# Kernel rows and their gradients by pairs of channels in a fused S4 convolution and gated FFN, forward and backward

## The chip, the core and the metric

The kernel runs on one core of one Trainium2 chip, as one program. The core has five engines, each with its own instruction queue: TensorE (PE, with its weight loads shown as PEld), VectorE (DVE), ScalarE (ACT), GpSimd (POOL) and SyncE (SP, which here only issues DMAs). The metric is the device time of one execution in microseconds; several executions are timed and the median is given. One further execution is recorded by the hardware profiler, and all rows of profiles and traces below come from that one.

## The reference

Inputs are a sequence `u` of 2048 tokens by 512 channels, the parameters of an S4 layer (`A`, `B`, `C` as real and imaginary parts, 512 channels by 128 states, `log_dt` and `Dskip` by channel), two FFN weights (512 x 1792 and 1792 x 512) and a gradient of the output. The outputs are the forward result and eleven gradients. Cut to what matters:

```python
xn = layernorm(u)
dt = exp(log_dt)[:, None];  dB = dt * (B_re + 1j*B_im)
P  = exp((dt * (A_re + 1j*A_im))[:, :, None] * arange(L))      # channel, state, time
K  = einsum("dn,dnl,dn->dl", C, P, dB).real                    # the kernel row of each channel
s  = irfft(rfft(xn padded) * rfft(K padded))[:L] + xn * Dskip  # a causal convolution
g  = silu(silu(xn @ w1) @ w2)
out = u + s * g
# and the gradients of out by u, A_re, A_im, B_re, B_im, C_re, C_im, log_dt, Dskip, w1, w2
```

For the change two parts matter: the kernel rows `K`, and on the way back the gradients by `A`, `B`, `C` and `dt` that come from the gradient of `K`.

## The kernel before, in words

All large products are bf16 with f32 sums in PSUM, a block of 128 partitions at a time. The convolution is done by DFTs on TensorE (a step of 128-point products at line 405, transposes at 415, a second step at line 425, and the way back at 440 and 453), the FFN by plain products (751, 768; backward 1149, 1169, 1202, 1231).

**Kernel rows.** The power of a state at time `e + 8 j` is the product of two, one of 32 powers `8 j` (tile `Y`) and one of 21 exponents `e` (tile `E`, `NE = 21`); times in between take the row of a neighbour when `KE` is filled. With the states on the partitions, the sum over states is then a matmul of `Y` (weights) by `E` times the coefficients (tile `W`). Channels are taken by four: the weights hold `(j, a)`, 32 x 4 = 128 columns, where `a` is the channel within the four, and the moving side holds `(e, a)`, 21 x 4 = 84 columns. Only the quarter in which both `a` agree is wanted. There are four terms (real and imaginary, two exponent halves), so `gen_kernel_rows` issues 16 products for every four fours of channels into one PSUM tile `ps_k` (128 x 336), and copies that to `Xr`. It does this for 4 blocks of 128 channels, 2 halves, 2 groups of 8 fours, 2 parts of a group: 512 products and 32 copies. Then `group` picks the wanted quarter: products with 0/1 matrices `SEL[kind, a]`, one for each `a`, summed over `a` into `ps_e`, which also moves rows between the 128 partitions where an exponent wraps. The rows are copied to `KE` and by DMA to the layout of the DFT (`Kb`).

**Their gradients.** `gen_ssm_fold` reads the gradient of the rows (four DMAs a block, one for each `a`), folds it with 0/1 matrices `FO` (line 953) and copies it with the last dimension repeated four times to `Gf`. `gen_ssm_v` multiplies `Gf` by a mask `MK` that leaves for each partition `(j, a)` the columns of its own `a` (`Gb`, 128 x 2688 elements), and multiplies the transposed powers `YT` by it: per four channels and per real or imaginary part one product of 168 columns into `ps_v` (line 998), four products into one PSUM tile of two banks, which is then copied to `Vb` (256 products, 64 copies). `gen_ssm_products` multiplies by `E` (`Tp`, line 1013), `gen_ssm_sums` adds over the exponents with an identity matrix (1031 to 1035), `gen_ssm_grads` turns the sums into the gradients.

**Order.** Every part is a Python generator that issues a few instructions and yields. Each has a letter, and a string `PLAN` of seven stages says which generator goes on next, so it sets the order of the instructions in every engine's queue: stage 1 set-up (begins at 0 us), stage 2 kernel rows `R`, powers `P` and `Q`, forward convolution `X` and `C`, FFN forward `F` (about 60 to 212 us), stages 3 and 4 the convolution backward and the FFN backward, stages 5 and 6 the gradients of the rows (`N`, `Y`, `V`, `T`, `S`, `Z`) beside the weight gradients (`t`, `w`, `v`), stage 7 the layer norm backward. `WAYS` says for each copy out of PSUM of a letter whether ACT (`A`) or DVE (`D`) does it (`k.ev`, lines 112 and 113). `SLOTS` says which buffer a tile takes. Products of a stage use PSUM pools `pf` (3 buffers), `pc` (2) and `pt` (1); `ps_k`, `ps_e` and `psS` share the one of `pt`, `ps_v` uses `pc`.

One form in this kernel already uses less than the full width of TensorE: the second DFT step (line 425) has weights of 64 columns and writes its results to partitions 0 to 63 and 64 to 127 in turn.

Of the kernel before, what the change touches and what calls it, by code (L numbers as in the profile page):

```python
# [18 lines left out]
P = 128  # L19
# [8 lines left out]
222127p33355553317511p333366565577077700071076676JJ17677p77747767676677F7FF777F6777477677FF77F77FFp77FF67766F667FF6F6FF8  # L28
4466666644468886685JJ8888/QFFFFFFJJXXXXFFFFXXPPFFXFXPXFPP9PFFFFFXXFFFXXPQFFQJXXQQQQQQXQJFPXPXQPQRXFFPPRRXRXXPFFFXRFRFRXR
PRQQQPQFFQQQQRFFXXQFQQRRRRPPXXFFFFFFFRRJRXFXRRRPPRUXXRRPXXXRRQRQQFQQFXXXRRRXRRQRRPRQQQQJFFQXXPPRFFFFFFPRRPPFFFCCCCCFXCFR  # L30
RRRCFFCFFFFFRFRCCQQQQQQFRRCRRCCQQQFFFQCCCCPFFFRRCCCCRRFQRCFXXXRRXPCCCRPCCQFCXPXFFQCRURFFXFRQQQCCXRCFQFFFCCQPQQFFFFCRRCQF
XFXPPRRXRRFXXXJXQRRXFRRCCXXPRRPPJJPRCRCXRPFQRCCCQXXPCJCCQFFFQQFFFRFCCPPFFCCQFRQFFQQXFQCXQFFCFFFRRRCFFCCRRCJCCRRCCCRCRCPC
RCRXXFFQRCRXXXQQCRCXRCCXCXRQQRRRRXRQRXQQXQQFXRXPFXXXFFFCJCPFRFPPCCCCFFRRPPFXRQRRRFFFXUFQQQFFXCCFCCFQFCRRCUCQCCCFRQQRCCQR
QFCQFCCRRCCRRRRRCCRCCRRCRCCCCRRFFFFCRCCCCCRRRCRRCCRC/FCCCCFFCCCCCFGGFGGCCCCCGGGGGGFGFGCCCCGGGGGFFCFFFFFCFCCFFGWGGCCCCHHF
FGGGCCCCCFGCCFFCCCCCWCCCCHWGGWWWCCCHHHHHWWCWWWCCWCCWDMWWWDGDDWWDWWDDDWLWWWWDWDDDLCLLLMMMMDDDWWDD/dDDaDaddDDdDsAAAEADDDDD
BAaBAAaABBDEaAAsADDDAsABBBAABBBoooAoAAABBBsAAAEDBBADBlDBDAlAlBBBBBxBDABBBBOAooAxxDDoBDBABoAAOBBEBOBOOOOOlldlxaBxxBooBBBo
sxOooBBBBDDDDxoxoxBdDaxBBDBAABBBdBBBDDAAaBBBBOBBBBBBAABBsAAAOADDDEDAAADBAADOOoBsOdOBABOBAoAoAAABBBDoxAOAOODBABosBBABDxDB
BAoOBDDDDAADDAAODxDDooodDAOOOdoBBaOBBOBoBBoOOdodDDxDEDxxBxaBBBsAAAOOaAABBABABBDBDAABDBDBoBoBBxxDOOExDDDsxAABBxBABBaBABBs
AAABBABBEOOOxOxBAABBBABBABAxBBBxxaaaBBBBBAsBBBBBBBBBBBBAAAxxBBBAAABBBBBAAAABBBABdBd/xxdAdNssxxsYaAsAAAAYYNAAAAAAAxxNNAAA
AAAAAAYAAAAAANNxVVVVAAxVVVVVVAATTVVxxVVxVVYxVVTYYxxxxNNNTTTTNSVVVVVVVYxSx/VTTSTSVTTVVVVVhhVVVSSVVVVVVVTTTYYttTtSthVTTNTT  # L40
# [31 lines left out]
d=DDADAAAA;  # L72
B=AADAADAAAAAADAAAAAAAAAAAAAAAAAADDADAAADAAAAAAAAAAAAAADDA;
x=ADADAAADDADADDAA;
V=ADDADDADADDADADAAAAAAADDAAAAADAAADAAAAAAAAAAADAAAAAAAAAAAAAAADAA;
w=DADDDDAAAAAAAA;
v=DADADDDAADDAAAAAAAAADAAADAAA"""

# [1366 lines left out]
```

## Time and profile before

| | us |
|---|---|
| median of 3 runs | 607.65 |
| lowest, highest | 607.44, 610.42 |
| the profiled execution | 606.76 |
| its span, first to last instruction | 605.0 |
| PE busy in it | 560.1 |
| DVE busy | 533.0 |
| ACT busy | 443.2 |
| POOL busy | 77.5 |

The mean TensorE clock granted in the span is 0.989 of full speed. A row of a group gives line, engine, operation, the tiles written and read, the shapes and the count, then busy time and the mean of one in ns, then the engine's idle time just ahead of them with what ended it. A row in order of time gives start and length in us of a series of equal instructions. Lengths of matmuls overlap, so their cost in a series is read from start to start. A row of a stretch gives its bounds, its length, and busy time with counts for PE, PEld, DVE, ACT and POOL, then clock, DMA share and GB/s.

### The profile page before, as it was taken

What the parts mean: (1) busy time and instruction counts of PE and PEld (TensorE: products, weight loads), DVE (VectorE), ACT (ScalarE), POOL (GpSimd) and SP (SyncE); (2) the same over time, 40 slices, a digit from 0 to 9 for tenths busy, and PEclk for the clock granted to TensorE, in tenths of its full rate; (3) what the DMA queues carried; (4) which work ended last, traced back from release to release, by engine and by line L of the source; (5) the groups of instructions that cost most, each with busy time, mean ns of one, the idle gap of its engine ahead of it and who ended that gap; (6) DMA issues with size and microseconds to landing.
All of it is one profiled execution on the core that took longest, in us unless ns stands there. A gap on an engine that the chain in (4) does not pass through costs nothing. (4 is left out here: it accounts for less than half of the span.)

```text
span 605.0 us, 14383 instructions
## 1 busy us (share of the span) xinstructions
PE 560.1 (93%) x5861; PEld 425.3 (70%) x5884; DVE 533.0 (88%) x906; ACT 443.2 (73%) x552; POOL 77.5 (13%) x171
## 2 busy tenths in 40 slices
PE   1597989999999989999999999999799999999995
PEld 1354758677777686786787767775787888795864
DVE  8989999999999889999998799568759889978894
ACT  7989989999998669998787864641575456434661
POOL 6211001010101120000000100000000202123121
PEclk9988999999999999999999999999999999999998
DMA  9896678676658598959877798797999999999993
GB/s 267 260 306 203 254 245 287 225 249 236 248 160 331 216 297 322 330 126 294 276 232 250 233 296 253 210 230 181 242 202 207 232 252 150 246 207 270 309 242 132
DMA packets 156066, 146.83 MB, mean 243 GB/s; under 512 B 79520, under 2 KB 133024, under 8 KB 152416
## 3 DMA queue, kind: packets, MB, share of 16 engines
q1 hardware_dynamic: 146688, 123.10, 72.1%
q0 software_dynamic: 6768, 19.93, 9.2%
q10 hardware_dynamic: 2544, 2.88, 1.5%
q8 instruction: 46, 0.75, 0.5%
q14 instruction: 20, 0.16, 0.1%
HBM read 63.44 MB, written 62.00 MB: 207 GB/s over the span
## 5 line engine op out<-in xcount | busy, mean ns | idle before, releaser
L112 ACT CAST dA<-ps_s 128x1024 bf16<-128x1024 f32 x86 | 86.3, 1037 | 7.6 <-PE ps_s L425 4.0
L751 PE MATMUL ps_h<-XT,W 128*128 128x256 bf16 x448 | 57.4, 279 | 6.2 <-ACT hT L112 4.6
L112 ACT CAST Vb<-ps_v 128x672 bf16<-128x672 f32 x49 | 34.1, 723 | 37.3 <-PE ps_v L998 32.7
L1149 PE MATMUL ps_da<-doT,W 128*128 128x256 bf16 x448 | 55.2, 273 | 1.2 <-ACT pd_s L112 1.1
L1013 DVE TENSOR_TENSOR Tp<-Vb,Eb 128x1344 bf16<-128x1344 bf16 x64 | 51.0, 850 | 5.9 <-ACT Vb L112 5.9
L768 PE MATMUL ps_o<-W,aT 128*128 128x512 bf16 x214 | 52.7, 399 | 1.1 <-issue 0.9
L112 ACT CAST dB<-ps_i 128x1024 bf16<-128x1024 f32 x41 | 41.1, 1031 | 16.4 <-PE ps_i L440 15.6
L751 PEld LDWEIGHTS <-W 128*128 128x128 bf16 x448 | 43.6, 100 | 12.9 <-issue 7.3
L1231 PE MATMUL ps_w<-dh_tok,xn 128*128 128x256 bf16 x448 | 51.8, 273 | 0.1
L1169 PE MATMUL ps_dx<-W,dhT 128*128 128x512 bf16 x224 | 50.8, 379 | 0.0
L1202 PE MATMUL ps_w<-YD,a_tok 128*128 128x512 bf16 x214 | 49.8, 379 | 0.5
L440 PE MATMUL ps_i<-I,sp_in 128*128 128x256 bf16 x384 | 47.3, 273 | 1.7 <-ACT dB L112 1.7
L1149 PEld LDWEIGHTS <-W 128*128 128x128 bf16 x448 | 42.8, 98 | 8.0 <-issue 2.8
L1231 PEld LDWEIGHTS <-xn 128*128 128x128 bf16 x448 | 43.2, 98 | 5.9 <-issue 0.5
L1152 DVE TENSOR_TENSOR dhT<-ps_da,dhT 128x512 bf16<-128x512 f32 x56 | 37.2, 684 | 10.3 <-PE ps_da L1149 7.3
L440 PEld LDWEIGHTS <-sp_in 128*128 128x128 bf16 x384 | 37.0, 98 | 8.9 <-DVE dB L113 1.9
L768 PEld LDWEIGHTS <-aT 128*128 128x128 bf16 x224 | 22.0, 102 | 29.3 <-issue 7.9
L1169 PEld LDWEIGHTS <-dhT 128*128 128x128 bf16 x224 | 21.3, 98 | 24.2 <-issue 1.2
L1202 PEld LDWEIGHTS <-a_tok 128*128 128x128 bf16 x224 | 21.5, 98 | 23.2
L466 DVE TENSOR_TENSOR cm<-sp_in,dA 128x2048 bf16<-128x2048 bf16 x24 | 29.3, 1219 | 4.9 <-DMA sp_in<-KXd 3.3
L425 PE MATMUL ps_s<-dB,F 128*64 128x512 bf16 x192 | 28.2, 388 | 3.8 <-ACT dB L112 2.1
L571 ACT ACTIVATE sn<-V 128x2048 bf16<-128x2048 int16 (+1 forms) x16 | 30.5, 1905 | 1.1 <-DVE V L567 1.1
(241 smaller groups left out, 1254.2 us busy)
## 6 DMA issues: line engine op xcount, KB each, us to landing
Yd<-YD SPq DMA_DIRECT2D x8, 1024.0 KB, 4.9
sp_in<-Ud SPq DMA_DIRECT2D x8, 1024.0 KB, 7.3
h_in<-Hd SPq DMA_DIRECT2D x14, 512.0 KB, 5.1
Ed<-E SPq DMA_DIRECT2D x8, 672.0 KB, 3.9
Eb<-Ed SPq DMA_DIRECT2D x8, 672.0 KB, 5.4
Hd<-hT POOLq DMA_DIRECT2D x8, 512.0 KB, 6.1
Ud<-dA SPq DMA_DIRECT2D x4, 1024.0 KB, 5.2
KXd<-dA SPq DMA_DIRECT2D x4, 1024.0 KB, 4.3
```

The lines of the kernel that those rows point to most:

```text
L112: return self.nc.scalar.copy(out=out, in_=in_)
L440: nc.tensor.matmul(out=ps[:, g], lhsT=Y[:, c, g0 + g, :], rhs=k.I2[:, c].rearrange("p c m -> p (c m)"), start=(c == 0), stop=(c == 1))
L466: TT(out=t2[:], in0=b[:, :, gs], in1=a[:, 1:2, gs].to_broadcast([P, 2, n, P]), op=ALU.mult)
L571: nc.scalar.activation(out=sn[:, 0:n], in_=low, func=ACT.Sin, scale=-2 * PI_LO / 2.0 ** PB)
L751: nc.tensor.matmul(out=ps[:, j], lhsT=k.W1[:, dk, ft * P:ft * P + P], rhs=XTv[:, :, dk, :], start=(dk == 0), stop=(dk == DK - 1))
L768: nc.tensor.matmul(out=ps[:], lhsT=aT[:, ft, t * P:t * P + P], rhs=k.W2[:, ft, :], start=(ft == 0), stop=(ft == FT - 1))
L1013: k.nc.vector.tensor_tensor(out=Tp[:, c, :, r ^ c].rearrange("p e (q w) a -> p q w e a", w=2), in0=Vb[:, :, c].rearrange("p q w (e a) -> p ...
L1149: nc.tensor.matmul(out=ps[:, j], lhsT=k.W2[:, ft, dk * P:dk * P + P], rhs=dTv[:, :, dk, :], start=(dk == 0), stop=(dk == DK - 1))
L1152: nc.vector.tensor_tensor(out=dh[:, i0:i0 + 2, :], in0=ps[:], in1=dh[:, i0:i0 + 2, :], op=ALU.mult)
L1169: nc.tensor.matmul(out=ps[:], lhsT=dhs[ft // 8][:, ft % 8, t * P:t * P + P], rhs=k.W1[:, :, ft * P:ft * P + P], start=(ft == 0), stop=(ft ...
L1202: nc.tensor.matmul(out=ps[:], lhsT=at[:, t, :], rhs=k.do[:, t, :], start=(t == 0), stop=(t == k.T - 1))
L1231: nc.tensor.matmul(out=ps[:], lhsT=k.xn[:, t, dk * P:dk * P + P], rhs=dh[:, t].rearrange("p j n -> p (j n)"), start=(t == 0), stop=(t == k ...
```

## The change

Channels are taken by two instead of four, in both directions.

In `gen_kernel_rows` the weights are now `(j, a)` with two values of `a`, 64 columns, and the moving side `(e, a)` has 42. Each old product becomes two, one for each pair `z` of the four channels, and these write to partitions 0 to 63 and 64 to 127 of the same PSUM tile. `ps_k` holds eight fours instead of four (128 x 336 again), so there are 1024 products and 16 copies. Half of the result is wanted instead of a quarter, so `SEL` has two matrices for each kind, and `group` issues half as many products. Since the partitions now hold `(z, j, a)`, the 0/1 matrices are built from a permuted identity `pairs`.

In the gradients the last dimension of `Gf`, `MK` and `Gb` is two, so `Gb` has 1344 elements instead of 2688. Each product of line 998 becomes two, one for each half `z` of the partitions (64 rows of the weights and of the moving side each, 84 columns), written to the two banks of `ps_v`. The copy to `Vb` has as many elements as before, with `z` reordered. `Vb`, `Tp`, `E` and `Y` have the same sizes with rows of two instead of four in the last dimension. The gradient of the rows is read by the same four DMAs to other partitions.

`PLAN`, `SLOTS` and `WAYS` are all new: the order of the whole program differs. Stage 2 has 611 letters instead of 626, stage 3 159 for 163, stage 4 467 for 466, stage 5 117 for 109, stage 6 397 for 405.

```diff
-R=AAAAAAADAADDADAAAAAAAAAAAAAAAADDDDDDDDAADAADAAAAADDAAAAADAAAAAADAAAAAAADAAAADDA;
+R=AAADAADDAADAAAAAAAAAAADDAADDDDADAAAAAAAADDDDAADAAAAAAAAAAADAADA;
...
-V=ADDADDADADDADADAAAAAAADDAAAAADAAADAAAAAAAAAAADAAAAAAAAAAAAAAAADAA;
+V=AADADAADADDADADAAADDADADAAADDDDDAADDAAAAAAADADAAAAAAAAAAAAAADDAA;
...
-F=AADAAAAAAAAADAAADAAAAAAAAAAADDAAAAAAADADAAAADAAADAAAAAAAADDAADADDDDDDDAA;
+F=AADAAAAAAAADDAAAAAAAAAAAAAAAAAAAAAAAADADAAAADAAADAAAAAAADDAAAAADDADDDDAA;
...
-    k.SEL = k.p1.tile([P, 4, 4, 128], BF16, name="SEL")
+    k.SEL = k.p1.tile([P, 4, 2, 128], BF16, name="SEL")
...
+    G.memset(w.pairs[:], 0.0)
+    G.affine_select(out=w.pairs[:], in_=w.pairs[:], compare_op=ALU.not_equal, fill=1.0,
+                    base=0, pattern=[[2, 32], [64, 2], [1, 2]], channel_multiplier=-1)
...
-            W = tbl.tile([P, 4, 8, NE, 4], BF16, name="W", tag="W", bufs=2)
+            W = tbl.tile([P, 4, 16, NE, 2], BF16, name="W", tag="W", bufs=2)
...
-            for u in range(2):
-                ps = k.pt.tile([P, 4, 84], F32, name="ps_k", tag="pt")
-                for q in range(4):
-                    for m in range(4):
-                        nc.tensor.matmul(out=ps[:, q], lhsT=Y[:, m % 2, q0 + 4 * u + q].rearrange("p j a -> p (j a)"),
-                                         rhs=W[:, m, 4 * u + q].rearrange("p e a -> p (e a)"), start=(m == 0), stop=(m == 3))
-                yield
-                qq = 16 * h + q0 + 4 * u
-                k.ev(Xr[:, :, :, qq:qq + 4], ps[:].rearrange("p q (e a) -> p a e q", a=4))
-                yield
+            ps = k.pt.tile([P, 8, NE * 2], F32, name="ps_k", tag="pt")
+            for q in range(8):
+                for m in range(4):
+                    for z in range(2):
+                        nc.tensor.matmul(out=ps[64 * z:64 * z + 64, q], lhsT=Y[:, m % 2, 2 * (q0 + q) + z].rearrange("p j a -> p (j a)"),
+                                         rhs=W[:, m, 2 * q + z].rearrange("p e a -> p (e a)"), start=(m == 0), stop=(m == 3))
+                if q % 4 == 3:
+                    yield
+            qq = 16 * h + q0
+            k.ev(Xr[:, :, :, qq:qq + 8], ps[:].rearrange("p q (e a) -> p a e q", a=2))
+            yield
...
-        n = len(terms) * 4
+        n = len(terms) * 2
...
-            for a in range(4):
+            for a in range(2):
                 nc.tensor.matmul(out=o, lhsT=k.SEL[:, kind, a], rhs=Xr[:, a, e0:e1, :], start=(i == 0), stop=(i == n - 1))
...
-    Gf = sb.tile([P, 32, NE, 4], BF16, name="Gf", tag="Gf", bufs=2)
+    Gf = sb.tile([P, 32, NE, 2], BF16, name="Gf", tag="Gf", bufs=2)
...
-            Gb = sb.tile([P, 16, 2, NE * 4], BF16, name="Gb", tag="Gb", bufs=2)
+            Gb = sb.tile([P, 16, 2, NE * 2], BF16, name="Gb", tag="Gb", bufs=2)
...
-                    nc.tensor.matmul(out=ps[:, u, 168 * c:168 * c + 168], lhsT=YT[:, c, q + u, :],
-                                     rhs=Gb[:, q0 + q + u].rearrange("p w x -> p (w x)"), start=True, stop=True)
-            yield
-            k.ev(Vb[:, q:q + 2].rearrange("p q c w x -> p q (c w x)"), ps[:, :, 0:336])
+                    for z in range(2):
+                        zs, x0 = slice(64 * z, 64 * z + 64), 168 * u + 84 * c
+                        nc.tensor.matmul(out=ps[:, z, x0:x0 + 84], lhsT=YT[zs, c, q + u, :],
+                                         rhs=Gb[zs, q0 + q + u].rearrange("p w x -> p (w x)"), start=True, stop=True)
+            yield
+            k.ev(Vb[:, 2 * q:2 * q + 4].rearrange("p (u z) c w x -> p z u (c w x)", z=2),
+                 ps[:, :, 0:336].rearrange("p z (u x) -> p z u x", u=2))
...
-        Tp = sb.tile([P, 2, NE, 2, 16, 4], BF16, name="Tp", tag="Tp", bufs=2)
+        Tp = sb.tile([P, 2, NE, 2, 32, 2], BF16, name="Tp", tag="Tp", bufs=2)
```

## The prediction

> **What bounds the kernel now.** I read the page first (busy shares, the span in slices), then busy time by stretch, then the groups and the order in time of the tiles that the change touches, then the waits. The page's shares:
>
> ```profile
> PE 560.1 (93%) x5861; PEld 425.3 (70%) x5884; DVE 533.0 (88%) x906; ACT 443.2 (73%) x552; POOL 77.5 (13%) x171
> PE   1597989999999989999999999999799999999995
> ```
>
> The share is an average over unlike stages, so the stretches decide (busy us of PE, weight loads, DVE, ACT, POOL):
>
> ```profile
> 90.00:120.00 30.00, 29.89 (x344) 22.23 (x343) 29.69 (x36) 29.94 (x38) 3.56 (x5) 1.00 0.72 257
> 120.00:150.00 30.00, 29.64 (x334) 22.68 (x336) 29.93 (x47) 29.80 (x36) 3.24 (x4) 1.00 0.68 239
> ...
> 420.00:450.00 30.00, 26.71 (x362) 22.46 (x362) 18.57 (x24) 16.80 (x24) 0.57 (x1) 1.00 0.96 222
> 450.00:480.00 30.00, 29.89 (x330) 23.11 (x330) 27.59 (x63) 17.25 (x23) 4.28 (x8) 1.00 1.05 218
> 480.00:510.00 30.00, 29.89 (x377) 25.55 (x377) 27.22 (x60) 17.27 (x28) 2.39 (x4) 1.00 0.95 208
> ```
>
> The kernel rows lie in the second stage (60 to 212 us). There PE, DVE and ACT are all full, so a gain on one alone is worth nothing; the stage gains what the least relieved of the three gains. Their gradients lie in the fifth and sixth stages (405 to 545 us). There PE alone is full and ACT is half idle; the longest wait there says the same, ACT waits for the gradient products of line 998:
>
> ```profile
> ACT Vb L112 <- PE ps_v L998: 32.7, 18, 6.4
> ```
>
> Next, what a matmul costs. Durations of single matmuls overlap, so I take start to start, from the order in time (start, us, line, shapes, count):
>
> ```profile
> 63.81 0.77 PE L639 MATMUL ps_k<-W,YD 128*128 128x84 bf16 x16
> 64.42 0.61 PE L405 MATMUL ps_s<-xn,TF 128*128 128x128 bf16 x8
> ...
> 433.75 0.74 PE L998 MATMUL ps_v<-Gb,YT 128*128 128x168 bf16 x8 [1.92 <-DVE Vb L113]
> 434.33 1.33 PE L1031 MATMUL psS<-Tp,ident 128*128 128x128 bf16 x21
> 435.50 0.22 PE L1033 MATMUL psS<-Tp,ident 128*128 128x64 bf16 x2
> ...
> 138.02 0.61 PE L453 MATMUL ps_i<-dB,TI 128*128 128x128 bf16 x8
> 138.56 0.14 PEld L425 LDWEIGHTS <-F 128*64 128x64 bf16 x4
> 138.56 0.62 PE L425 MATMUL ps_s<-dB,F 128*64 128x512 bf16 x4
> 139.12 0.47 PE L639 MATMUL ps_k<-W,YD 128*128 128x84 bf16 x8
> ```
>
> Sixteen products of 84 columns take 64.42 - 63.81 = 0.61 us, 38 ns each; eight of 168 columns 0.58 us, 73 ns; 21 of 128 columns 1.17 us, 56 ns. So a column costs (73 - 38)/84 = 0.42 ns and a product 3 ns more; 512 columns cost 216 ns. Line 425, the second DFT step, is half-width already, in pairs on the two halves of the columns. Its four 512-column products occupy 0.56 us, not 4 x 0.216 = 0.86: two run side by side. But the switch is dear. From the first L453 to the first L639 are 1.10 us; 8 x 0.056 + 2 x 0.216 = 0.88 are work, and 0.21 us go into entering and leaving the half-width form (the last L453 ends its columns at 138.47, L425 starts at 138.56). This 0.21 us is paid once for each unbroken run of half-width work, and it is a PE loss in stages where PE is full.
>
> **Part 1: kernel-row products (stage 2).** 512 products of 84 columns cost 512 x 38 ns = 19.4 us. After it there are 1024 of 42 columns, as 512 pairs. A pair streams 42 x 0.42 + 3 = 20 ns, if both halves run at once. It needs two loads of 64 weights; the four loads of L425 above last 0.14 us, a single one 0.11, so a pair's loads follow the other's by some 25 to 28 ns. I take the load as the limit, 28 ns a pair: 14.3 us, a gain of 5.1. Ends: 20 ns (gain 9.2), and no overlap at all, 56 ns (28.7 us, a loss of 9.3). L425 is the nearest row.
>
> **Part 2: selections (stage 2).** Per channel block 4 products of 512 columns, 4 of 160, 8 of 224, 8 of 128: 0.86 + 0.28 + 0.77 + 0.45 = 2.36 us, four blocks 9.4 us. Half remain: gain 4.7 us.
>
> **Part 3: switches in stage 2.** I followed the order strings letter by letter, by which letter issues which products. Before there are 21 runs of half-width work in this stage (all L425). After there are 29, since many row products sit next to L425 or to each other: 8 x 0.21 = 1.7 us lost. PE in this stage: -5.1 - 4.7 + 1.7 = -8.1 us.
>
> **Part 4: copies out of PSUM in stage 2.** These are the groups now:
>
> ```profile
> L112 ACT CAST Xr<-ps_k x28: 431/460/545, 65.0 to 202.5; 128x336 bf16<-128x336 f32 x28
> L113 DVE CAST Xr<-ps_k x4: 494/498/506, 82.0 to 197.8; 128x336 bf16<-128x336 f32 x4
> ```
>
> 32 become 16 of the same 336 elements. The new assignment strings leave 1 of 16 on DVE, and move 4 of the forward copies of 512 elements (0.68 us on DVE, 0.63 on ACT) from DVE to ACT. DVE: -3 x 0.50 - 4 x 0.68 = -4.2 us; ACT: -13 x 0.46 + 4 x 0.63 = -3.5 us. So PE could give 8, the other two about 4: the stage gains 4 us (end: 8, if PE alone counted).
>
> **Part 5: DVE products with rows of two instead of four.** Counts and elements stay for W (32 x 0.85 us), the powers (48 x 0.95) and Tp (64 x 0.85). 1344 elements in rows of four take 0.85 us, 2048 in long rows 1.22 (group of line 466): 0.53 ns an element and 0.14 us each for both, so short rows cost nothing now. I take 0. The other end is one element at a time: +0.70 us for each W and Tp.
>
> **Part 6: gradient products (stages 5, 6).** 256 products of 168 columns cost 256 x 73 = 18.7 us. After: 512 of 84 columns on half of the rows each, in pairs: 256 x 38 = 9.7 us, gain 9.0. No row of the trace has a product on half the rows; the other end is that the pairs run in turn, 512 x 38 = 19.5, a loss of 0.8. I take the pair, since L425 shows it for the column halves. The switch has no row either for this form; I take L425's 0.21 us (ends 0 and twice that). The order strings have 33 runs of these products between full-width work, 5 and 28, where there were none: 33 x 0.21 = 6.9 us lost. PE: -9.0 + 6.9 = -2.1 us. The Trainium skill, TensorEngine Tiling (Array Packing), Key Properties, says that changing the tiling mode drains the TensorE, whichever mode is entered. No run here shows it for row halves; L425's 0.21 us agrees for column halves. Without that rule and that row the sum would be lower by 8.6 us.
>
> **Part 7: masked rows and copies (stages 5, 6).**
>
> ```profile
> L1013 DVE TENSOR_TENSOR Tp<-Vb,Eb 128x1344 bf16<-128x1344 bf16 x64 | 51.0, 850 | 5.9 <-ACT Vb L112 5.9
> L988 DVE TENSOR_TENSOR Gb<-Gf,MK 128x2688 bf16<-128x2688 bf16 x8 | 12.4, 1546 | 0.0
> L956 ACT CAST Gf<-G 128x2048 bf16<-128x2048 f32 x4 | 7.5, 1867 | 6.3 <-PE G L953 6.3
> ```
>
> Gb falls to 1344 elements, Tp's size: 8 x (1.55 - 0.85) = -5.6 us on DVE. The new string puts 22 of 64 Vb copies on DVE instead of 15: 7 x 0.85 = +6.0. Net 0 for DVE, and ACT, with 13 of 30 us idle, loses some 9 us of work. Covered by PE; if PE fell by over 10 us here, DVE (27.5 of 30) would be next. Waiting for a smaller Gb is shorter; I count 0.
>
> **Part 8: the rest.** POOL gets one memset and one selection more (0.20 + 0.29 us, as for the identity) and two SEL copies for four (2.37 us now), with 1.13 us of idle behind them: 0. DMA counts and bytes stay. The order of all engines' queues is new, SP's and POOL's too; its worth cannot be read from the trace. I take 0 and keep 4 us to both sides: the worst idle of PE in a 30 us stretch after 60 us is 3.3 (420 to 450).
>
> **Sum.** -4 - 2.1 = -6.1 us. The profiled execution took 606.8 us (span 605.0), so 600.7; the median shown, 607.65, stands 0.9 above it, so 601.5.
>
> **Rivals.**
> (a) Row halves run in turn (slower). Place: the runs of L998 in stages 5 and 6. Price: +0.8 + 6.9 there, -4 in stage 2: +3.7, so 611.4. It turns slower than before when a pair costs over 62 ns instead of 38 (256 x 24 ns = 6.1). For it: no row shows this form. Against: column halves overlap. With the column halves in turn too, stage 2's PE gains nothing: +9.3 - 4.7 + 1.7 = +6.3, in all +14, so 622.
> (b) A floor per product. Five products of 32 and three of 64 columns took 399.11 - 398.90 = 0.21 us, 27 ns each:
>
> ```profile
> 398.90 0.38 PE L953 MATMUL G<-GE,FO 128*128 128x32 bf16 x8
> 399.11 0.38 PE L1149 MATMUL ps_da<-doT,W 128*128 128x256 bf16 x2
> ```
>
> If each half of a pair pays 25 ns, the row products cost 1024 x 25 = 25.6 us, +6.2 instead of -5.1: stage 2's PE +3.2, with some slack -0 to +3, in all 605.5 to 608.5, no change. Against: L425's two halves start together. The Trainium skill, TensorE: Matmul & The Clock Gate, section "Wait — 56ns, not 53.3ns?", has this floor as about 25 ns from start to start however few the columns; the eight products agree for full width.
> (c) The new order gives 4 us back, or hides the gain in other waits: 605.
> (d) Switches for row halves are cheap and stage 2 is worth PE's 8: 592 to 598.
> (e) Rows of two halve DVE's rate: +0.70 x 96 = 67 us at least, 675. Against: no cost for rows of four.
>
> **How the numbers follow.** Two timings of this kernel differ by up to 3 us of 607, so 0.5% (604.6 to 610.7) is what can be told. Forecast (598 to 604.6) 0.40; (d) 0.12; (b) and (c) together 0.22; (a) row halves alone 0.13, half of it within 0.5%; (a) with both, 0.08; (e) and worse 0.05. Faster 0.52, same 0.28, slower 0.20. The range 592 to 615 leaves out both-in-turn and (e), 0.13, and a tail below. The forecast's own range is 598 to 604.6.
>
> **What would show it.** Row products: 64 of them in 0.9 us (32 x 28 ns), starts of two within some ns. A hole of about 0.1 us ahead of and behind each run of half-width products. Gb at 0.85 us, W and Tp still at 0.85. L998: eight products in 0.15 us plus 0.21. Wrong, if eight take 0.3 or more, if W takes over 1 us, or if DVE and ACT idle in stage 2.

## The result and the profile after

The changed kernel takes 640.84 us (median of 4 runs, 637.45 to 642.35) beside 607.86 for the kernel before on the same chip: ratio 1.053, interval 1.048 to 1.058. It is slower by 33 us; the forecast was 601.5, the range ended at 615. The profiled execution took 642.35 us, its span 640.6.

The page after, busy shares and TensorE's slices:

```profile
PE 568.8 (89%) x6604; PEld 423.8 (66%) x6604; DVE 567.5 (89%) x908; ACT 429.1 (67%) x534; POOL 79.3 (12%) x171
PE   1697799988898999999999999995998988979995
```

VectorE has 34.5 us more to do (567.5 for 533.0) in two instructions more. Something that was counted at no cost has become dearer. The groups of VectorE, as in the prediction's part 5 and 7 (line, tiles, form, count, busy us, mean ns):

```profile
L1022 DVE TENSOR_TENSOR Tp<-Vb,Eb 128x1344 bf16<-128x1344 bf16 x64 | 78.4, 1336 | 0.3
...
L638 DVE TENSOR_TENSOR W<-E,CT 128x1344 bf16<-128x1344 bf16 x32 | 26.3, 858 | 0.0
L603 DVE TENSOR_TENSOR E<-sn,mag 128x2048 bf16<-128x2048 bf16 x8 | 19.1, 2394 | 2.6 <-DMA mag<-Md 2.6
...
L603 DVE TENSOR_TENSOR YD<-sn,mag 128x896 bf16<-128x896 bf16 x8 | 7.9, 992 | 0.0
...
L603 DVE TENSOR_TENSOR E<-sn,mag 128x640 bf16<-128x640 bf16 x8 | 7.0, 881 | 0.0
L994 DVE TENSOR_TENSOR Gb<-Gf,MK 128x1344 bf16<-128x1344 bf16 x8 | 6.8, 848 | 0.0
```

Four groups of the kernel before, of which the prediction shows none:

```profile
L633 DVE TENSOR_TENSOR W<-E,CT 128x1344 bf16<-128x1344 bf16 x32 | 26.1, 847 | 0.0
...
L598 DVE TENSOR_TENSOR E<-sn,mag 128x2048 bf16<-128x2048 bf16 x8 | 9.7, 1216 | 0.7 <-DMA mag<-Md 0.7
...
L598 DVE TENSOR_TENSOR YD<-sn,mag 128x896 bf16<-128x896 bf16 x8 | 4.9, 616 | 0.0
...
L598 DVE TENSOR_TENSOR E<-sn,mag 128x640 bf16<-128x640 bf16 x8 | 4.1, 510 | 0.0
```

`Tp` went from 850 to 1336 ns with the same 1344 elements: 64 x 0.486 = 31.1 us (27.4 by the busy time of the group, 78.4 for 51.0, since neighbours overlap a little). `E` of 2048 elements went from 1216 to 2394, `E` of 640 from 510 to 881, `YD` from 616 to 992 and `H` of 384 from 349 to 430, eight of each: 9.4 + 3.0 + 3.0 + 0.6 = 16.0 us. `W`, of as many elements as `Tp`, did not move (847 to 858). What the slow ones have in common is how they store. `Tp[:, c, :, r ^ c]` is written in the order group, `w`, exponent, channel: two elements, then a step to the next exponent, 256 bytes on. Before it was four elements, then the step. `E`, `Y` and `H` are written in the same broken way, with steps of 84, 128 and 12 bytes by the shapes of their tiles; `W` is written without a break.

**Where it fell.** By the first `ps_k` the changed kernel is 2.1 us behind (65.9 for 63.8), from there to the last `ps_k` it loses 12.3 (150.8 for 138.5), in the stages between it gains 2.4, and from the first `ps_v` to the end it loses 23.6 (219.1 for 195.5).

In the kernel-row stage seven of the eight sets of `E`, `Y` and `H` cost 14.0 us more, and the stage grew by 12.3: nearly one for one, since VectorE was busy 135.3 of its 138.5 us before. The eighth set, 2.0 us, lies ahead of the first `ps_k`, which is 2.1 late.

In the late stages `Tp` cost 31 us more and the kernel lost 24, though the prediction took TensorE for the bound there. Three stretches of 30 us (columns as in the prediction: bounds, PE, PEld, DVE, ACT, POOL, clock, DMA share, GB/s):

```profile
435.00:465.00 30.00, 23.10 (x373) 19.79 (x373) 26.98 (x27) 12.12 (x18) 0.34 (x1) 0.94 0.89 192
465.00:495.00 30.00, 26.95 (x317) 19.24 (x314) 28.23 (x59) 11.80 (x17) 4.45 (x9) 0.92 0.96 216
...
525.00:555.00 30.00, 27.27 (x356) 19.87 (x352) 29.55 (x61) 15.46 (x24) 5.58 (x10) 0.94 0.77 155
```

VectorE is now the fullest, and TensorE has holes, times in which it does nothing. TensorE's waits from 421.5 us to the end:

```profile
PE ps_v L1006 <- DVE Vb L112: 8.4, 5, 3.6
PE ps_v L1006 <- ACT Vb L111: 4.1, 4, 2.5
```

One of them in the order of time shows the whole mechanism:

```profile
442.94 4.81 DVE L1022 TENSOR_TENSOR Tp<-Vb,Eb 128x1344 bf16<-128x1344 bf16 x4
...
444.43 0.48 PE L1006 MATMUL ps_v<-Gb,YT 64*128 64x84 bf16 x16
...
447.58 0.85 DVE L112 CAST Vb<-ps_v 128x672 bf16<-128x672 f32 x1
448.49 0.48 PE L1006 MATMUL ps_v<-Gb,YT 64*128 64x84 bf16 x16 [3.58 <-DVE Vb L112]
```

TensorE has filled both places of `ps_v` at 444.9. One of the two copies stands on VectorE, in its queue behind four `Tp` that now take 4.81 us; the next product needs that place, and TensorE waits 3.58 us for it. What follows such a hole is slow too (the same columns as the stretches above):

```profile
444.43:448.49 4.06, 0.47 (x18) 0.37 (x17) 4.01 (x4) 1.04 (x2) 0.00 (x0) 1.00 1.04 285
448.90:452.98 4.08, 4.08 (x47) 3.98 (x44) 4.08 (x5) 0.72 (x1) 0.00 (x0) 0.58 0.93 222
```

In the hole TensorE works 0.47 of 4.06 us; in the 4 us behind it the granted clock is 0.58. After the first `ps_v`, TensorE's holes sum to 21.2 us (before 4.5; a hole is counted from the latest end of a matmul to the next start), and 115 of the 128-column sums start 80 to 200 ns apart instead of 56 (before none), 5.7 us more in all. 16.7 + 5.7 = 22.4 of the 23.6.

**What the prediction said of TensorE.** The row products and the gradient products in order of time:

```profile
65.92 1.19 PE L644 MATMUL ps_k<-W,YD 128*64 128x42 bf16 x64
67.04 2.31 PE L757 MATMUL ps_h<-XT,W 128*128 128x256 bf16 x10
...
484.31 1.28 PE L1044 MATMUL psS<-Tp,ident 128*128 128x128 bf16 x20
485.52 0.48 PE L1006 MATMUL ps_v<-Gb,YT 64*128 64x84 bf16 x16
485.93 1.92 PE L1240 MATMUL ps_w<-dh_tok,xn 128*128 128x256 bf16 x16
```

Sixty-four row products take 67.04 - 65.92 = 1.12 us with their end, 35 ns a pair; inside the series the pairs start 32 ns apart, the two of a pair 3 ns. Sixteen gradient products take 485.93 - 485.52 = 0.41 us: eight pairs of 38 ns are 0.30, the rest is the switch back. The switch in shows ahead of them: 20 x 0.056 = 1.12 us of sums end their columns at 485.43, and `ps_v` starts 0.09 later.

### The profile page after: what moved, and what is told of

The parts are those of the page before. It is cut to its first block, busy times and chain, and to the rows that moved or that the text cites. A ratio compares the mean times of both kernels' runs of the same rounds, so it can differ in the third digit from the quotient of the medians.

```text
span 640.6 us, 15839 instructions
## 1 busy us (share of the span) xinstructions
PE 568.8 (89%) x6604; PEld 423.8 (66%) x6604; DVE 567.5 (89%) x908; ACT 429.1 (67%) x534; POOL 79.3 (12%) x171
## 5 line engine op out<-in xcount | busy, mean ns | idle before, releaser
L1022 DVE TENSOR_TENSOR Tp<-Vb,Eb 128x1344 bf16<-128x1344 bf16 x64 | 78.4, 1336 | 0.3
L757 PE MATMUL ps_h<-XT,W 128*128 128x256 bf16 x448 | 61.2, 293 | 10.1 <-DVE hT L112 4.2
L757 PEld LDWEIGHTS <-W 128*128 128x128 bf16 x448 | 45.7, 105 | 20.2 <-issue 12.3
L111 ACT CAST Vb<-ps_v 128x672 bf16<-128x672 f32 x42 | 29.5, 724 | 35.3 <-PE ps_v L1006 25.2
L111 ACT CAST dB<-ps_i 128x1024 bf16<-128x1024 f32 x42 | 41.4, 1024 | 12.7 <-PE ps_i L445 12.6
L1158 PEld LDWEIGHTS <-W 128*128 128x128 bf16 x448 | 42.7, 98 | 7.2 <-issue 2.1
L1202 ACT ACTIVATE a_tok<-pt_t 128x1024 bf16<-128x1024 bf16 x28 | 28.0, 1024 | 12.0 <-PE pt_t L133 11.8
```

Of the source, the lines that this page charges most:

```text
L111: return self.nc.scalar.copy(out=out, in_=in_)
L757: nc.tensor.matmul(out=ps[:, j], lhsT=k.W1[:, dk, ft * P:ft * P + P], rhs=XTv[:, :, dk, :], start=(dk == 0), stop=(dk == DK - 1))
L1022: k.nc.vector.tensor_tensor(out=Tp[:, c, :, r ^ c].rearrange("p e (q w) a -> p q w e a", w=2), in0=Vb[:, :, c].rearrange("p q w (e a) -> p ...
L1158: nc.tensor.matmul(out=ps[:, j], lhsT=k.W2[:, ft, dk * P:dk * P + P], rhs=dTv[:, :, dk, :], start=(dk == 0), stop=(dk == DK - 1))
```

## Experiments

Three readings stood against each other. **S**: VectorE is slower when it stores rows of two elements with a longer step between them, and nothing else is lost. **R**: it is not the stores but reading in such rows. **O**: the rows have nothing to do with it, and the new order of issue, the row halves or a busier memory make the instructions longer.

### The rows by themselves

A kernel of its own, timed in one execution, runs series of six VectorE products of 1344 elements, each series with another layout, and six series of 24 TensorE products of 128 columns.

```diff
+ V(out=D[:, 0:2688]... 'p e (n a) -> p n e a', a=4, in0=S[:, 0:1344]..., in1=R[:, 0:1344]...)   # rows of four, step 256 bytes
+ V(out=D[:, 0:2688]... 'p e (n a) -> p n e a', a=2, in0=S[:, 0:1344]..., in1=R[:, 0:1344]...)   # rows of two, step 256 bytes
+ V(out=D... 'p (n s) -> p n s', n=672)[:, :, 0:2], ...)                                          # rows of two, steps of 8, 12, 16, 32, 64 bytes
+ V(out=D[:, 0:1344]... 'p (n e a) -> p e n a', n=32, e=21, in0=S[:, 0:1344]..., in1=R[:, 0:1344]...)   # rows of two, step 84 bytes, as E
+ V(out=D[:, 0:1344]..., in0=Bg[:, 0:2688]... 'p e (n a) -> p n e a', a=2, ...)                   # a source in rows of two
```

> Leaves the whole computation out and writes zeros; it holds series of six VectorE products of 1344 bf16 elements that differ only in how the elements lie, and series of 24 TensorE products of 128 columns that differ in how the moving side lies. Theory S (stores of two elements that do not touch the next are slow): all contiguous 0.85 us, destination in rows of two 1.3 to 1.5 us at every stride over 2 elements, rows of four and eight 0.85, sources in rows of two with a contiguous destination 0.85. Theory R (rows of two are slow as sources): the series with scattered sources takes 1.3 us or more, the scattered destination 0.85. TensorE: 56 ns each for the contiguous side; no theory for rows of two, 56 if reads of 4 bytes cost nothing and 112 if they halve the rate.

Eight groups of VectorE and two series of TensorE (L48 no breaks; stores in rows of four, L50, and of two, L52, 256 bytes apart; stores in rows of two every 8 bytes, L56, every 16, L58, and every 84, L76; one source in rows of two, L63, and both, L64; TensorE reading rows of two, L72, and of four, L73, with the series behind that ends it; for VectorE the mean of one in ns stands last before the bar, for TensorE start and length in us):

```profile
L64 DVE TENSOR_TENSOR Dx<-Bgx,Bhx 128x1344 bf16<-128x1344 bf16 x6 | 9.8, 1637 | 0.3
L76 DVE TENSOR_TENSOR Dx<-Sx,Rx 128x1344 bf16<-128x1344 bf16 x6 | 9.4, 1560 | 0.2
...
L52 DVE TENSOR_TENSOR Dx<-Sx,Rx 128x1344 bf16<-128x1344 bf16 x6 | 8.1, 1353 | 0.2
...
L58 DVE TENSOR_TENSOR Dx<-Sx,Rx 128x1344 bf16<-128x1344 bf16 x6 | 8.1, 1348 | 0.2
...
L63 DVE TENSOR_TENSOR Dx<-Bgx,Rx 128x1344 bf16<-128x1344 bf16 x6 | 7.8, 1294 | 0.3
...
L56 DVE TENSOR_TENSOR Dx<-Sx,Rx 128x1344 bf16<-128x1344 bf16 x6 | 5.2, 860 | 0.2
L50 DVE TENSOR_TENSOR Dx<-Sx,Rx 128x1344 bf16<-128x1344 bf16 x6 | 5.2, 859 | 0.2
...
L48 DVE TENSOR_TENSOR Dx<-Sx,Rx 128x1344 bf16<-128x1344 bf16 x6 | 5.1, 858 | 3.3 <-POOL Rx L47 3.1
```

```profile
27.83 3.52 PE L72 MATMUL ps_rtwo<-Bgx,identx 128*128 128x128 bf16 x24
31.16 1.63 PE L73 MATMUL ps_rfour<-Bgx,identx 128*128 128x128 bf16 x24
32.62 3.52 PE L74 MATMUL ps_rsplit<-Bgx,identx 128*128 128x128 bf16 x24
```

The 1336 ns of `Tp` are here without the kernel around them: stores in rows of two take 1.35 us, in rows of four 0.86, as without breaks. Every 8 bytes costs nothing, every 12 bytes makes 1.06 us, and ten series with steps from 16 to 1024 bytes take 1.29 to 1.37 us, but for one: the step of `E`, 84 bytes, takes 1.56. Why that one is dearer is open. Per element the additions are 0.15, 0.33 and 0.52 ns for steps of 12, 128 and 84 bytes; in the changed kernel `H`, `Y` and `E`, which have these steps, cost 0.21, 0.42 and 0.58 more. One source in rows of two costs as much as the result (1.29), where S expected 0.85; both sources take 1.64. So storing and reading in rows of two are both slow, and in the changed kernel it is the stores that lie so. ScalarE hardly slows down: its copy takes 1364 ns in rows of two and 1312 without breaks. TensorE does: 24 products in rows of two, 84 bytes apart, take 31.16 - 27.83 = 3.33 us, 140 ns each, more than the 112 that half the rate would make; in rows of four they take 1.46 us, 60 each, and in one piece 56.

### The stores of Tp, and of Tp and E, without breaks

The changed kernel, with the same products on the same sources, writing their 1344 (and 2048, 640) elements one behind the other.

```diff
-            k.nc.vector.tensor_tensor(out=Tp[:, c, :, r ^ c].rearrange("p e (q w) a -> p q w e a", w=2),
+            k.nc.vector.tensor_tensor(out=Tp[:].rearrange("p c e r x a -> p (c e r x a)")[:, 1344 * (2 * c + (r ^ c)):1344 * (2 * c + (r ^ c)) + 1344]...,
...
-            parts = ((E[:, :, :, 0:16, :], 0, 16),)
+            parts = ((fl(E[:])[:, 0:2048], 0, 16),)
```

> The kernel after, with the products Tp stored one after the other instead of two by two 256 bytes apart. The sums that follow then add the wrong elements, so the gradients by A, B, C and dt are left wrong; the count and size of all instructions stay. Theory S: Tp falls from 1.34 to 0.85 us, DVE loses 31 us of work, and of the 33 us that the kernel after is slower the 22 lost behind 420 us come back: 617 to 621 us. Theory R: nothing changes, 641. Theory O (the new order of the program is the worse one, the slow DVE lies beside other work): Tp may fall, the time stays above 630.

> As tp_flat, and the powers E also stored one after the other, which leaves the kernel rows and all that follows from them wrong. Theory S: E falls from 2.39 and 0.88 to 1.22 and 0.51 us, 12 us less of DVE work in the second stage, where DVE is full; 606 to 611 us. Theory O: above 625. If it comes to 598 to 605, the rest of the prediction stands.

`Tp` alone: 617.64 us (616.76 to 619.46), ratio to the kernel before 1.015 (1.012 to 1.017), so 23 us of the 33 are gone. Its group on the page:

```profile
L1022 DVE TENSOR_TENSOR Tp<-Vb,Eb 128x1344 bf16<-128x1344 bf16 x64 | 51.0, 851 | 1.5 <-DMA Eb<-Ed 1.1
```

`Tp` and `E`: 608.00 us, ratio 0.9995 (0.997 to 1.002); `E` of 2048 elements takes 1220 ns, and all of the loss is gone, with the new order, the row halves, the switches and the copies still in place (and `Y` and `H` still stored in rows of two). O falls. From the first `ps_v` to the end it is 194.2 us, 1.3 less than before; TensorE's holes there are 6.1 us and no sum is slow.

### One thing alone, in the kernel before

The other direction: the kernel before, whole, with only the stores of `Tp` in rows of two. Since one instruction cannot say this, each product is cut in four, and a control is cut in four without changing the rows.

```diff
-            k.nc.vector.tensor_tensor(out=Tp[:, c, :, r ^ c].rearrange("p e (q w) a -> p q w e a", w=2), ...
+            for w, z in ((0, 0), (0, 2), (1, 0), (1, 2)):     # the control: (0, 0), (0, 4), (1, 0), (1, 4), and z:z + 4 of the groups
+                k.nc.vector.tensor_tensor(out=Tp[:, c, :, r ^ c].rearrange("p e (q w) a -> p q w e a", w=2)[:, :, w, :, z:z + 2],
+                                          in0=Vb[:, :, c, w].rearrange("p q (e a) -> p q e a", a=4)[:, :, :, z:z + 2],
+                                          in1=E[:, ec, q0:q0 + 8, :, z:z + 2], op=ALU.mult)
```

> The kernel before with each of the 64 products into Tp cut into four of 336 elements (by w and by half of the groups), rows of four as they were. The control for the next run: only the number of instructions changes, 256 instead of 64. Each should take 300 to 350 ns by the slope between the E products of 640 (510 ns) and 1344 (850 ns): 11 to 35 us more on VectorE, 612 to 632 us.

> The kernel before with each of the 64 products into Tp cut into four of 336 elements by w and by pair of channels, so that each writes rows of two elements 256 bytes apart (and reads rows of two every 8 bytes); Tp itself and all else is the kernel before. Against the run with rows of four, the same number of instructions on the same elements. Theory S: each product takes 0.12 us more (0.36 ns an element, from 1336 against 850 ns for 1344), 31 us more on VectorE in all, and 20 to 31 us more time than with rows of four. Rival O (the loss of the changed kernel comes from its order of issue, from the row halves or from a busier memory, not from the rows of two): the same duration within 5% and the same time within 3 us.

The group of the control, and of the run in rows of two:

```profile
L1014 DVE TENSOR_TENSOR Tp<-Vb,Eb 128x336 bf16<-128x336 bf16 x256 | 64.4, 327 | 5.0 <-ACT Vb L112 4.9
```

```profile
L1014 DVE TENSOR_TENSOR Tp<-Vb,Eb 128x336 bf16<-128x336 bf16 x256 | 80.1, 461 | 3.7 <-ACT Vb L112 3.7
```

461 for 327 ns, 0.134 us each (0.12 expected), 34 us over 256 by count times mean. The times are 613.38 (ratio 1.008, 1.007 to 1.010) and 625.33 (1.027, 1.025 to 1.028): 12 us apart. That is S, but the size was missed: 20 to 31 were expected. Where the rest of the 34 us went shows in the totals: VectorE's busy time in the whole kernel is 546.1 us in the control and 560.4 with rows of two, 14 more. Such short instructions overlap (256 x 0.327 is 84 us, the control's busy time for them 64.4), and the longer ones cover more of each other; the expectation had added their lengths. In rows of two the group is busy for 80.1 us, near the 78.4 of the 64 whole products of the changed kernel. The edit has one more difference: the sources are read in rows of two every 8 bytes, which no run times by itself on VectorE. The stores alone would make 0.12 of the 0.134 us.

### The same change with sources in rows of two

An attempt to mend it: turn the loops of the `E` and `Y` products so that they store without breaks and read in rows of two, and lay `Tp` out so that it is stored without breaks and TensorE reads rows of two when it sums.

```diff
-            TT(out=eq(o), in0=qe(sn[:, i0:i1]), in1=qe(m), op=ALU.mult)
+            for c in range(2):
+                TT(out=o[:, c], in0=turn(sn[:, i0:i1, c]), in1=turn(mag[:, x0 + i0:x0 + i1, :]), op=ALU.mult)
...
-            nc.tensor.matmul(out=psS[:, 0:2], lhsT=k.ident[:], rhs=flat(Tp[:, 0, e]), start=(e == 0), stop=False)
+            nc.tensor.matmul(out=po(psS[:, 0:2]), lhsT=k.ident[:], rhs=Tp[:, 0, :, :, e], start=(e == 0), stop=False)
```

> The kernel after with the whole computation, but with long stores: the products E and Y are made in two halves with the loops turned, so that the sources and not the destination lie in rows of two, and Tp is laid out as the product runs, so that TensorE reads rows of two in the sums. Theory S: Tp 0.85 us, E two of about 0.68 us; 24 to 32 instructions more on DVE cost 4 us of the 16 gained in the second stage. 607 to 613 us if TensorE reads rows of two as fast; 38 us of sums more, 630 or above, if it reads them at half the rate. Theory R: E and Y stay slow.

676.96 us, ratio 1.112 (1.109 to 1.114), worse than the change itself. `Tp` takes 852 ns again, but the `E` halves, with both sources in rows of two, take 1228 ns for 1024 elements (2394 for 2048 in the changed kernel), where 680 was expected, and the sums start 140 ns apart instead of 56. The break costs wherever it is put.

### Rows of four kept, pairs kept

Then the pairs can be taken out of rows of four. In `quad` TensorE reads two channels of four from `W` every 8 bytes, which the first experiment shows to be free for VectorE; in `rows_only` a pair is channels `z` and `z + 2`, so weights and moving side are every second column, and the gradients are those of the kernel before.

```diff
-                        nc.tensor.matmul(out=ps[64 * z:64 * z + 64, q], lhsT=Y[:, m % 2, 2 * (q0 + q) + z]..., rhs=W[:, m, 2 * q + z]...
+                        nc.tensor.matmul(out=ps[64 * z:64 * z + 64, q]..., lhsT=Y[:, m % 2, 2 * (q0 + q) + z]..., rhs=W[:, m, q, :, 2 * z:2 * z + 2]
...
+                        nc.tensor.matmul(out=ps[64 * z:64 * z + 64, q], lhsT=Y[:, m % 2, q0 + q].rearrange("p j a -> p (j a)")[:, z::2],
+                                         rhs=W[:, m, q].rearrange("p e a -> p (e a)")[:, z::2], start=(m == 0), stop=(m == 3))
```

> The changed kernel with the powers E, the rows W, Vb, Tp, the sums and the last gradients put back into rows of four, and everything else of the change kept: half-width products in pairs, one copy for two, half the selections and masks. TensorE reads a pair of channels out of W as rows of two every 8 bytes, and the copies of ps_v write rows of two every 8 bytes. Only Y and H are still stored in rows of two far apart. Theory S (the loss is VectorE storing rows of two far apart, and nothing else): Tp 850 ns and E 1216 ns as before the change, 606 to 611 us, as with Tp and E contiguous (608.0). Rival Q (rows of two every 8 bytes are slow for TensorE too): pairs of kernel-row products at 60 to 80 ns instead of 32, 615 to 625 us. Rival N (the pairs themselves lose time, by their switches or by the new order of issue): above 612 us with Tp and E at the old durations and the pairs at 32 ns.

> The kernel-row half of the change alone, with every product of VectorE in the layout of the kernel before: channels z and z+2 make a pair, so TensorE takes every second column of Y as weights and every second column of W as the moving side; half-width products side by side, one copy for two, half the selections, the order of issue of the changed kernel; the gradient half (row halves, masks, Vb, Tp, sums) is the kernel before. Theory S: all products of VectorE as before the change (Tp 850, E 1216, E of 640 510, Y 616 ns), from the first ps_v to the end 195 us as before, and the kernel-row stage shorter by what the prediction's parts 1 to 4 left of 4 us after the new order: 602 to 608 us in all. Rival N (the pairs or the new order lose time by themselves): 609 to 613 us with the same durations. Rival Q (columns taken every second one slow TensorE down): pairs at 60 to 80 ns instead of 32, 613 to 625 us.

> The kernel-row half alone as before (run rows_only), but with the order of issue and the choice of copying engine of the kernel before from the output projection's backward part to the end, where the program is that of the kernel before; the order of the changed kernel is kept only up to there. In rows_only the first ps_v stood at 407.1 us (409.5 before) and from there to the end it took 199.9 us (195.5 before). Theory W (the kernel rows in pairs are worth some 2 us, and the order of the changed kernel, 22 copies of ps_v on VectorE among it, costs the gradients of the kernel before some 4): first ps_v at 407 to 408, 195 to 196 from there, 603 to 606.5 us beside 608, ratio 0.993 to 0.998. Rival P (in rows_only the two stretches differ by the way one run falls, and the pairs are worth nothing): ratio 0.999 to 1.003.

`quad`: 607.60 us, ratio 0.998 (0.995 to 1.000). `rows_only`: 609.39, 1.001 (1.000 to 1.003). `rows_late`, with the order of the kernel before in the late stages: 606.17, 0.998 (0.995 to 1.000). `Tp` takes 851 to 853 ns in all three and `E` 1.22 us (in `quad`, `Y` and `H` still lie in rows of two: 947 and 432 ns). Q, that pairs every 8 bytes or every second column slow TensorE down, falls: the pairs of row products start 32 ns apart in all three, as in the changed kernel. `rows_only` missed the range of S, 602 to 608, and fell into that of N, in which the new order or the pairs lose time by themselves. By these ratios the change without its stores lies between 1.5 us faster and 0.7 slower, which this kernel's timings hardly tell from nothing, where the prediction gave it 6. `rows_only` loses in the late stages what it wins before (199.9 us from the first `ps_v`, 195.5 before), and there its program is that of the kernel before in the new order, with the new choice of copying engine; the order and choice of the kernel before give part of that back (197.5), and the other 2.0 are not explained.

### Where the gain of the kernel-row stage stayed

The prediction let that stage gain 4 us, the least of the three engines' reliefs. Two runs take half of VectorE's products into `W` out of it, in the kernel before and in `rows_late`.

```diff
-                TT(out=W[:, m:m + 2].rearrange("p m q e a -> p (m q) e a"), in0=e, in1=ct, op=ALU.mult)
+                if m == 0:
+                    TT(out=W[:, m:m + 2].rearrange("p m q e a -> p (m q) e a"), in0=e, in1=ct, op=ALU.mult)
```

> The kernel before with half of the 32 products into W left out (the rows of the imaginary half are read from the first half instead, so kernel rows and what hangs on them are wrong): 16 x 0.85 = 13.6 us less for VectorE in the stage of the kernel rows; TensorE and ScalarE do all they did. That stage takes 138.5 us, VectorE busy 135.3, TensorE 133.8, ScalarE 132.7. Theory D (VectorE bounds the stage and TensorE stands 4 to 5 us behind it): 3 to 5 us off, 603.5 to 605.5 beside 608.5. Rival T (TensorE's order bounds it): within 2 us of before.

> The run rows_late (kernel rows in pairs, all layouts of VectorE as before) with the same half of the products into W left out, results wrong in the same way. The stage takes 139 us in rows_late with TensorE busy 128.6, VectorE 133.4, ScalarE 128.9. Theory D (the pairs freed 4 to 5 us of TensorE, and VectorE, which they freed of 1.4 us only, held the end of the stage): with VectorE out of the way the stage can fall to what TensorE and ScalarE need, 6 to 9 us off, 597 to 600, and the distance to the run of the kernel before with the same products left out is 4 to 7 us instead of the 2 between rows_late and before. Rival T (TensorE's work or its order bounds the stage in both): the distance stays 1 to 3 us.

The stage in the kernel before, then in `rows_late`, then in the two with half of `W`, in the same 138.2 us:

```profile
63.80:202.00 138.20, 133.54 (x1612) 101.88 (x1620) 135.30 (x180) 132.38 (x170) 14.23 (x18) 1.00 0.69 250
```

```profile
63.80:202.00 138.20, 128.63 (x2030) 96.20 (x2030) 133.40 (x176) 128.93 (x157) 14.41 (x18) 1.00 0.69 244
```

```profile
63.80:202.00 138.20, 134.96 (x1628) 102.06 (x1625) 125.32 (x166) 133.72 (x173) 14.27 (x18) 1.00 0.69 250
```

```profile
63.80:202.00 138.20, 130.59 (x2103) 97.80 (x2102) 125.42 (x163) 132.16 (x163) 13.70 (x18) 1.00 0.70 250
```

607.19 us (ratio 0.997, 0.995 to 0.999) and 604.03 (0.993, 0.991 to 0.995): 3.2 apart (2.7 by the ratios), where `rows_late` and the kernel before are 2.4 apart (1.4). The times that D expected, 603.5 to 605.5 and 597 to 600, did not come, and the distance lies at the upper edge of T's 1 to 3, so the runs speak rather for T and do not settle it. What the stretches do show: with VectorE relieved by 8 to 10 us, TensorE and, in the paired kernel, ScalarE (132.2 of 138.2) are as full as before, and the stage shortens by 1.6 us in the one and 4.5 in the other (first to last `ps_k`: 136.9 for 138.5, 134.9 for 139.4). These are single traces: in `rows_only`, in the same order up to there as `rows_late`, the stage took 137.7 us, so that the 4.5 could as well be 2.8. That VectorE held back some of the gain in the paired kernel is therefore not shown, and how much each of the three keeps is open.

### Copies of ps_v all on ScalarE

The prediction counted seven more copies on VectorE as covered. Three runs take all of them off it: the kernel before, `quad` and the changed kernel.

```diff
-V=AADAADAADDADADADAAADDADADAAADDDDDAADDAAAAAAADADAAAAAAAAAAAAAAADDAA;
+V=AAAAAAAAAAAAAAAAAAAAAAAAAAAAAAAAAAAAAAAAAAAAAAAAAAAAAAAAAAAAAAAA;
```

> The control for quad_act: the kernel before with all 64 copies of ps_v on ScalarE, 15 of them off VectorE (-12.8 us on VectorE, +10.8 on ScalarE). From the first ps_v to the end VectorE is busy 161.4 of 195.5 us before, TensorE 184.5. Theory V: 2 to 4 us off, 604 to 606. Rival T: the same within 2 us.

> The run quad with all 64 copies of ps_v on ScalarE (22 of them on VectorE in the changed kernel, 15 before). It takes 22 x 0.85 = 18.7 us from VectorE and gives ScalarE 22 x 0.72 = 15.9 us; from the first ps_v to the end VectorE was busy 159.4 of 197.2 us in quad, ScalarE 92.5. Theory V (the prediction's part 7: these copies lie on VectorE's path): 2 to 6 us off, 602 to 606. Rival T (that stretch is TensorE's, busy 183.1 of 197.2): the same within 2 us. Below nothing: ScalarE's copies come one behind the other with the sums' copies, and TensorE waits for ps_v's place: 1 to 4 us more.

> The changed kernel with all 64 copies of ps_v on ScalarE instead of 42, nothing else. In it, from the first ps_v (421.5 us) to the end (640.6), VectorE is busy 184.6 of 219.1 us, TensorE stands still for 21 us in all where before it stood for 4.5, and most of that in ps_v, waiting until a copy on VectorE behind four products into Tp of 1.34 us has emptied its place. Theory H (the slower Tp costs time by what queues behind it on VectorE): without copies in that queue TensorE's waits for VectorE's Vb go, VectorE has 18.7 us less to do: 6 to 16 us off, 625 to 635. Rival B (the stage simply takes as long as VectorE's chain of Tp needs, copies or not; or the copies only wait on ScalarE instead): within 4 us of 640.8. In the run quad, with Tp at 0.85 us, the same edit cost 3 us.

The kernel before: 608.34 us, ratio 1.001 (0.998 to 1.003), no change. `quad`: 610.55, 1.004 (1.001 to 1.006), 3 us worse than with 22 on VectorE. The changed kernel: 631.38, 1.036 (1.033 to 1.040), 9.5 us better. TensorE's waits in it:

```profile
PE pt_g L1103 <- DVE gout L1076: 4.8, 3, 2.1
PE ps_v L1005 <- ACT Vb L110: 4.4, 8, 0.8
```

The 8.4 us of waiting for `Vb` on VectorE are gone, TensorE's holes are 15.9 us instead of 21.2, and 21 sums are slow instead of 115. So the copies on VectorE cost nothing that can be seen as long as `Tp` is fast, and 9.5 us beside a slow one; in the profiled executions the stretch from the first `ps_v` to the end falls from 219.1 to 207.6 us, 11.5 of the 23.6 lost there. How much of that is the queue and how much the 18.7 us that VectorE no longer has to do, the run does not part. A new wait appears as well: VectorE's `Tp` now stands 20.1 us for the copies on ScalarE.

## Why the prediction was wrong

**Part 5 is the step that failed.** It took 0 for rows of two, by arguing from rows of four, which cost nothing, to rows half as long. Its other end, 0.70 us for each `W` and `Tp`, was above the truth for `Tp` (0.49) and wrong for `W` (0.01), because it put the cost on the length of the last dimension. What counts is whether the next row follows: `W` has rows of two in its shape, but is stored in one piece, and so is its source `E` read; of `CT` it reads the same pair 21 times over, which costs nothing either. The powers on the list (48 x 0.95) did not move (953 to 957 ns for 948 to 953). The products that did, the ones that make `E`, `H` and the first rows of `Y` from `sn` and `mag`, were not on the list at all. Of the signs that it named, `W` over 1 us did not come, and `Tp` still at 0.85 failed. Rival (e) named this mechanism, at 0.05 and "67 us at least"; it came to 47 us on VectorE and 33 in all. The text that spoke against it, "no cost for rows of four", was true and did not bear on rows of two: none of the rows that the prediction shows had one, so the cost should have been bounded by the far end and kept in the range.

A rule that speaks against this step was there to be weighed. The Trainium skill, SBUF — State Buffer, section "Door 1: The DMA port swizzle (why `[64,N]` ≈ `[32,N]`)", says that the memory has lines of 16 bytes and that a pattern needs two hits or more in a line to run at full rate. The runs agree with it on which steps are slow, if a piece of two bf16 elements is one hit: every 8 bytes (two in a line) 860 ns, every 12 (some lines with one) 1056, every 16 and more (one in a line) 1286 to 1368. The 1560 ns at 84 bytes, also one in a line, it does not explain. The Trainium skill, Vector Engine (DVE) Microarchitecture Reference, section "5.2 Measured stream behaviour on trn2 (trn3 not measured)", asks for two 4-byte words side by side, which tells rows of four from rows of two as the runs do, but would make the step of 8 bytes slow; there the 860 ns decide against it.

**Part 1 held.** 32 ns a pair, 35 with the ends, against 28: 16.4 us for 512 pairs, a gain of 3.0 of the 5.1. Rival (b)'s floor of 25 ns for each product, from the Trainium skill, TensorE: Matmul & The Clock Gate, section "Wait — 56ns, not 53.3ns?", does not hold for products on two halves: they start 3 ns apart. Rival (c), the order that takes the gain back, is near what is left once the stores are mended.

**Part 3 and 6 held.** 33 runs of `ps_v`, a pair every 38 ns, and 0.19 us for switching in and out (0.09 ahead, some 0.10 behind) where 0.21 was borrowed from the column halves. The rule of the Trainium skill, TensorEngine Tiling (Array Packing), Key Properties, that a change of the tiling mode drains TensorE is borne out for row halves too, and these 0.19 us are its price here. With the stores mended the late stages gain 1.3 us in `tp_e_flat` and 0.8 in `tp_flat`; 2.1 were forecast. `quad`, also with a fast `Tp`, takes 1.6 us longer there than the kernel before (197.1 for 195.5), so a gain of this size is not told from the spread of single traces. Rivals (a), row halves in turn, and (d), cheap switches, fell.

**Part 2 held** (48 selections instead of 96, of the same shapes). **Part 4 held over the whole stage and not up to the last `ps_k`.** Over the whole stage the copies on VectorE come to 4.8 us less in the changed kernel (4.2 forecast) and those on ScalarE to 4.3 less (3.5). But VectorE gets part of its relief only behind the last `ps_k`. Ahead of it three `Xr` copies go (-1.5) and three of the forward ones (-2.0), and one of 1024 elements moves over to it (+1.3), by its position in a string with as many letters `D`. In the stretches above, `rows_late` beside the kernel before, VectorE loses 1.9 us (133.40 for 135.30), ScalarE 3.5 and TensorE 4.9. By the prediction's own rule, the least of the three, that would have given 1.9 instead of 4; at the first `ps_v`, `rows_only` and `rows_late` are 2.4 and 2.0 us ahead. That fits, but the two runs with half of `W` do not confirm the rule.

**Part 7** had `Gb` right (848 ns for 0.85) and its seven copies covered, as long as `Tp` is fast; the sentence on the cover named the wrong end of it. It looked at what would happen if TensorE fell by 10 us, not if VectorE's other work in that queue rose, though VectorE was busy 27.2 and 27.6 of 30 us in two of the three stretches there already.

**Part 8**, the new order, was given 0 with 4 to both sides: in `rows_only` the late stages, whose program is that of the kernel before, took 199.9 us in it for 195.5, and the old order gave 2.4 of these back. These 2.4 are within the 4.

## What to carry to other kernels

When a layout is cut finer, look at each operand of each instruction for the length of the piece that lies in one run, not at the last dimension of the tile; where no row of the trace has pieces that short, time one instruction by itself before trusting the longer ones. On an engine that also empties another engine's buffers, a slow instruction can cost time through the other engine's wait behind it, even in a stage that the other engine seems to bound. And where three engines are within 5% of full in a stage, a saving on one alone is worth little (10 us off VectorE shortened the stage by 1.6), so read what each one is relieved of, up to the end of that stretch.

## What the runs showed of the hardware

- VectorE, two sources and one result of bf16, 1344 elements: 0.86 us with the result in pieces of four elements or more, or of two elements every 8 bytes; 1.06 for two every 12 bytes; 1.29 to 1.37 for two with steps of 16 to 1024 bytes from piece to piece, and 1.56 with 84. One source in pieces of two, 64 or 256 bytes apart, takes 1.28 to 1.29, both sources 256 bytes apart 1.64. With its result in pieces of two, 256 bytes apart, a copy on VectorE goes from 0.51 to 0.74 us, one on ScalarE from 1.31 to 1.36.
- TensorE's moving side of 128 columns: 56 ns in one piece, 60 in pieces of four, 140 in pieces of two 84 bytes apart. Single columns taken every second one (`rows_only`) and pairs every 8 bytes (`quad`) cost the row products nothing that can be seen.
- Half-width products on the two column halves start 3 ns apart and a pair of 42 columns follows the last in 32 ns; on the row halves a pair of 84 columns takes 38 ns. Entering and leaving either form costs 0.19 to 0.21 us together.
- After a hole of 3.6 us on TensorE the granted clock was 0.58 for the next 4 us, and most of the 128-column products in them came 107 ns apart. A kernel that starts cold shows the same: in the kernel of rows by themselves 32 products of 128 columns came 107 ns apart, and 56 from then on.
